# Four operands and 32 bytes: moving the MLP's right operands to another place within 64 bytes

## The chip, the cores and the metric

The kernel runs on one core of a Trainium2 chip. The metric is the device time of one execution in microseconds; the kernel before took 1090.73 us, the median of 3 runs (1088.52 to 1092.98). A profile of one further execution shows what each engine did.

## The reference, cut to what matters

Attention with mixing over heads before and after the softmax, then a block of a low-rank mixing over tokens and an MLP:

```python
B, H, S, D = 4, 12, 448, 64          # attention
scores = q @ k.T / sqrt(D)
scores = einsum('bhij,hg->bgij', scores, w_pre)
attn   = softmax(scores)
attn   = einsum('bhij,hg->bgij', attn, w_post)
x = (attn @ v) as [B, S, 768]
u  = x + (x.T @ U @ V).T             # U 448x32, V 32x448
out = u + relu(u @ w_ch1) @ w_ch2    # w_ch1 768x3072, w_ch2 3072x768
```

U, V and the MLP's weights arrive as 64-bit floats, all else as 32-bit floats.

## The kernel before

The attention works on 16 units of tokens, four for each batch. A unit's scores are made by L381 from k and q, copied out of PSUM into one of three s buffers, and sent by a DMA (the relay, L388) into a tile t that has heads and tokens side by side, where L412 mixes the heads. Softmax, the second mixing (L447) and the product with v (L488, L496) follow, and the result is gathered in acc, one tile for each batch.

The low-rank step transposes acc (L677), multiplies by U (L694, 8 matmuls of 256 columns) and by V (L708, 2 matmuls of 448 columns). Its operands are full-rate 32-bit floats (float32r), split into a high and a low part. The sum u is split likewise into uh and ul, one pair of tiles for each batch.

The MLP takes the hidden dimension in 24 pieces f of 128 and the batches b one after the other. For each (f, b) the up step (L750) makes 18 matmuls: for each of 6 pieces of 128 model channels, low weights by uh, high weights by ul, high weights by uh. Each has 128x128 weights and a right operand of 448 columns, and each has its own weight load. ReLU's result is split into hh and hl (L755, L759), and the down step (L770) makes 3 matmuls for each hidden piece and each 128 output channels, which VectorE adds to acc (L773). 24 x 4 x 18 = 1728 matmuls are up, as many are down. The weights of the next f are loaded, narrowed from 64 to 32 bits by ScalarE, VectorE and GpSimd through kr and tmp buffers, and split meanwhile.

A planner in the kernel (class Plan) simulates the engines with its own costs and due times and writes out the order of all steps; from the third hidden piece on the order of the MLP is written by hand (`lines`). Neither looks at addresses.

SBUF is filled from two sides. Pools of the left side lie one behind another from the bottom, those of the right side from the top downwards, and a pool that is opened after others were closed takes their place. Every tile takes a multiple of 32 bytes in each partition, nearly all of them a multiple of 64. In the built program the right side's first buffer ends 32 bytes below a multiple of 64, and so kr, tmp1, k, u of batches 0 and 1, w0, u of batch 2, h, w0's second buffer, w1 and u of batch 3, which follow each other on that side, all start at 32 mod 64 (at 224 mod 256 too). The tiles of the low-rank step on the left (xh, xl, t3, u4, v4) start at 0 mod 64. The pools are opened by small steps without an engine, for instance:

```python
def open_qk(eng):
    qk_ctx.close()
    for b in range(2):
        open_u(b, "right")
    pool(whole, "w0_0", 1, "right")
```

Tile names in the rows: uh, ul, hh, hl are the right operands; w0h, w0l the up weights, w1h, w1l the down weights; xl, xh with u, and v with t, are the low-rank step's; bank is PSUM.

Of the kernel before, what the change touches and what calls it, by code (L numbers as in the profile page):

```python
# [8 lines left out]
F32 = mybir.dt.float32  # L9
# [233 lines left out]
def build(tc, q2, kt, vj, wpre_in, wpost_in, u_in, v_in, ident, w1j, w2, out, show=None):  # L243
    nc = tc.nc
    whole, tail_ctx, a_ctx, mix_ctx, t1_ctx, t0_ctx, qk_ctx = (ExitStack() for _ in range(7))
    sb = {}

    def pool(ctx, name, bufs, side="left", **kw):
        sb[name] = Pool(ctx.enter_context(tc.tile_pool(name=name, bufs=1, side=side, **kw)), plan.where)
        return sb[name]  # L250
# [26 lines left out]
        pool(mix_ctx, n, BUFS[n])  # L277
    pool(t1_ctx, "t1", 1)
    pool(t0_ctx, "t0", 1)
    for n in ("kr", "tmp1"):  # L280
        pool(whole, n, BUFS[n], "right")
    for n in ("k", "q", "s"):
# [239 lines left out]

    uh, ul = {}, {}

    def open_u(b, side):
        p = pool(whole, f"u{b}", 1, side)
        uh[b], ul[b] = (p.tile([128, KC, S], F32R, e) for e in ("uh", "ul"))
# [5 lines left out]
    def open_qk(eng):  # L533
        qk_ctx.close()
        for b in range(2):
            open_u(b, "right")
        pool(whole, "w0_0", 1, "right")

    def open_t0(eng):
        t0_ctx.close()  # L540
        open_u(2, "right")

    def open_t1(eng):
# [2 lines left out]

    def open_mix(eng):
        mix_ctx.close()
        pool(whole, "w0_1", 1, "right")

    def open_a(eng):
# [2 lines left out]

    def open_tail(eng):
        tail_ctx.close()
        open_u(3, "right")

    plan.add("open_qk", [(None, 0)], open_qk, 0, [("relay", nu - 1, h) for h in range(H)])
    plan.add("open_t0", [(None, 0)], open_t0, 0, ["open_qk"] + [("premix", k) for k in range(first[nu - 2] // 2, (first[nu - 1] + 1) // 2)])  # L560
    plan.add("open_t1", [(None, 0)], open_t1, 0, ["open_t0", ("premix", NC // 2 - 1)])
    plan.add("open_mix", [(None, 0)], open_mix, 0, ["open_t1", ("postmix", NC // 2 - 1)])
    plan.add("open_a", [(None, 0)], open_a, 0, ["open_mix"] + [("av", nu - 2, p) for p in (0, AV)])
    plan.add("open_tail", [(None, 0)], open_tail, 0, ["open_a"] + [("av", nu - 1, p) for p in (0, AV)])

    count = [0]
# [225 lines left out]
    for f in range(KF):  # L792
# [8 lines left out]
        for b in range(B):  # L801
# [9 lines left out]
            n = 1 if (f, b) == (KF - 1, B - 1) else 2  # L811
# [103 lines left out]
```

## Time and profile before

| what | value |
|---|---|
| median of 3 runs | 1090.73 us |
| the profiled execution | 1100.28 us |
| its span, first to last instruction | 1098.5 us |
| mean granted TensorE clock | 0.992 of 2.4 GHz |
| TensorE matmul busy | 1059.1 us |
| VectorE, ScalarE, GpSimd busy | 666.5, 408.4, 271.9 us |
| matmuls at L750 and L770 | 1728 each |

Matmuls overlap in the array, so that the duration of one (368 ns) is longer than the time from one start to the next; that time is read from a count of matmuls in a window, or from a group of the chain of waits divided by its count.

### The profile page before, as it was taken

How to read it: one execution, taken by the hardware profiler on the slowest of the kernel's cores; microseconds unless marked ns; L12 is line 12 of the kernel's file. 1: busy time of each engine (PE TensorE's matmuls, PEld its weight loads, DVE VectorE, ACT ScalarE, POOL GpSimd, SP SyncE). 2: the span in 40 equal slices, each digit the busy share in tenths (PEclk: the TensorE clock that was granted, in tenths of full speed). 3: DMA queues.
4: the chain of work that ended last, by engine and by line, in shares of the span. 5: the costliest groups of instructions: out<-in, count | busy, mean ns of one | idle time of the engine just before them, and what ended most of it. 6: DMA issues, size and time to landing. Idle time of an engine off the chain costs nothing.

```text
span 1098.5 us, 28397 instructions
## 1 busy us (share of the span) xinstructions
PE 1059.1 (96%) x12120; PEld 874.2 (80%) x12120; DVE 666.5 (61%) x1076; ACT 408.4 (37%) x852; POOL 271.9 (25%) x398
## 2 busy tenths in 40 slices
PE   4798999999999999999999999999999999999998
PEld 1365666665666899999999999999999999999997
DVE  0574564565688687665665666565666566566634
ACT  2786677677768721222112212212221211221200
POOL 3131111111224522232222222222222222222200
PEclk8899999999999999999999999999999999999999
DMA  7665646635755211221122212111211211221105
GB/s 277 191 187 171 196 128 193 200 119 167 213 198 163 82 31 44 58 58 58 44 58 58 58 44 58 56 46 58 58 48 53 58 44 57 58 58 44 44 1 200
DMA packets 52270, 108.11 MB, mean 98 GB/s; under 512 B 5056, under 2 KB 38320, under 8 KB 51632
## 3 DMA queue, kind: packets, MB, share of 16 engines
q1 hardware_dynamic: 52144, 106.30, 31.4%
q8 instruction: 95, 1.56, 0.6%
q14 instruction: 31, 0.25, 0.1%
HBM read 57.91 MB, written 7.08 MB: 59 GB/s over the span
## 4 chain that ended last, share of the span: by engine, by line
PE 89%; DMA 4%; ACT 3%; DVE 2%; issue 2%; SPq 0%; POOL 0%; ACTq 0%; DVEq 0%
PE bank L750 33%; PE bank L770 33%; PE bank L447 6%; PE bank L488 5%; PE bank L381 5%; PE bank L412 5%; DMA t<-s 3%; ACT e L422 2%; PE bank L496 1%; DVE mx L417 1%; PE bank L677 1%; PE bank L694 1%; ACT s L299 1%; DMA k<-in_kt 0%; ACT a L299 0%
## 5 line engine op out<-in xcount | busy, mean ns | idle before, releaser
L773 DVE TENSOR_TENSOR acc<-acc,bank 128x896 f32<-128x896 f32 (+1 forms) x153 | 163.5, 1070 | 173.5 <-PE bank L770 172.9
L755 ACT ACTIVATE hh<-bank 128x448 fp32r<-128x448 f32 x96 | 52.4, 546 | 492.2 <-PE bank L750 312.2
L750 PE MATMUL bank<-uh,w0l 128*128 128x448 f32 x576 | 212.2, 368 | 0.0
L770 PE MATMUL bank<-hh,w1l 128*128 128x448 f32 x576 | 212.1, 368 | 0.0
L770 PE MATMUL bank<-hl,w1h 128*128 128x448 f32 x576 | 211.9, 368 | 0.0
L770 PE MATMUL bank<-hh,w1h 128*128 128x448 f32 x576 | 211.9, 368 | 0.0
L750 PE MATMUL bank<-uh,w0h 128*128 128x448 f32 x576 | 211.9, 368 | 0.0
L750 PE MATMUL bank<-ul,w0h 128*128 128x448 f32 x576 | 211.9, 368 | 0.0
L610 POOL TENSOR_TENSOR a<-a,x 128x384 f32<-128x384 f32 (+2 forms) x98 | 98.6, 1006 | 422.6 <-PE bank L750 381.2
L417 DVE TENSOR_REDUCE mx<-bank 128x2 f32<-128x896 f32 x90 | 97.7, 1088 | 69.5 <-PE bank L412 63.7
L447 PEld LDWEIGHTS bank<-wr,e 60*64 60x64 f32 x5040 | 89.4, 135 | 45.8 <-issue 31.9
L422 ACT ACTIVATE e<-bank,mx 128x448 f32<-128x448 f32 x180 | 113.3, 642 | 13.0 <-DVE mx L417 9.2
L770 PEld LDWEIGHTS bank<-hh,w1l 128*128 128x128 f32 x576 | 108.1, 188 | 11.1 <-DVE acc L773 0.3
L770 PEld LDWEIGHTS bank<-hh,w1h 128*128 128x128 f32 x576 | 108.1, 188 | 10.9
L750 PEld LDWEIGHTS bank<-uh,w0l 128*128 128x128 f32 x576 | 108.1, 188 | 10.9
L750 PEld LDWEIGHTS bank<-uh,w0h 128*128 128x128 f32 x576 | 108.1, 188 | 10.9
L770 PEld LDWEIGHTS bank<-hl,w1h 128*128 128x128 f32 x576 | 108.1, 188 | 10.8
L750 PEld LDWEIGHTS bank<-ul,w0h 128*128 128x128 f32 x576 | 108.1, 188 | 10.8
L381 PE MATMUL bank<-k,q 64*64 64x448 f32 (+1 forms) x768 | 96.1, 569 | 15.5 <-ACT s L299 9.0
L759 DVE SCALAR_TENSOR_TENSOR hl<-bank,hh 128x448 fp32r<-128x448 f32 x96 | 59.9, 624 | 81.3 <-ACT hh L755 81.3
L447 PE MATMUL bank<-wr,e 60*64 60x60 f32 x5040 | 93.3, 219 | 8.9 <-issue 6.6
L412 PE MATMUL bank<-t,wpre 64*64 64x448 f32 x720 | 87.6, 557 | 8.8 <-DMA t<-s 5.8
(61 smaller groups left out, 1105.1 us busy)
## 6 DMA issues: line engine op xcount, KB each, us to landing
t<-s SPq DMA_DIRECT2D x192, 210.0 KB
kr<-in_w1j SPq DMA_DIRECT2D x48, 384.0 KB
kr<-in_w SPq DMA_DIRECT2D x48, 384.0 KB
v<-in_vj SPq DMA_DIRECT2D x4, 1536.0 KB
q<-in_q SPq DMA_DIRECT2D x32, 186.0 KB
out<-acc SPq DMA_DIRECT2D x9, 448.0 KB
k<-in_kt SPq DMA_DIRECT2D x4, 672.0 KB
k<-in_kt SPq DMA_DIRECT2D x4, 448.0 KB
```

Of the source, the lines that this page charges most:

```text
L381: eng.matmul(o[at, i, :S], lhsT=q[d, p, at], rhs=k[d, p, :], start=True, stop=True)
L412: eng.matmul(o[64 * j:64 * j + 64, i, :S], lhsT=wpre[64 * i:min(64 * i + 64, QW)], rhs=tt[u % 2][64 * i:min(64 * i + 64, QW), n, :], start ...
L417: eng.tensor_reduce(out=mx, in_=T["pre", k][:, :, :S], axis=AX.X, op=ALU.max, negate=True)
L422: eng.activation(out=e[:, i], in_=T["pre", k][:, i, :S], func=ACTF.Exp, bias=T["mx", k][:, i:i + 1], accum_out=sm[:, i:i + 1])
L447: eng.matmul(d, lhsT=e[64 * j:64 * j + HALF, i, x * KB:x * KB + KB], rhs=wr[64 * j:64 * j + HALF, i].rearrange("p (g m) -> p g m", m=MH), ...
L488: eng.matmul(main[i * D:(i + 1) * D, c, :n], lhsT=v[:, p + c, i, x, :], rhs=a[:, x * H + 2 * (p + c) + i, :n], start=(c == 0 and x == 0), ...
L610: eng.tensor_tensor(out=f32(a), in0=f32(a), in1=f32(x), op=ALU.add)
L750: eng.matmul(ps, lhsT=w[:, c * 128:(c + 1) * 128], rhs=u[:, c, :], start=(i == 0), stop=(i == 3 * KC - 1))
L755: eng.activation(out=hh, in_=T["up", f, b], func=ACTF.Relu)
L759: eng.scalar_tensor_tensor(out=hl, in0=T.pop(("up", f, b)), scalar=0.0, in1=f32(T["hh", f, b]), op0=ALU.max, op1=ALU.subtract)
L770: eng.matmul(ps[:, j, :S], lhsT=w[:, (c + j) * 128:(c + j + 1) * 128], rhs=h, start=(i == 0), stop=(i == len(todo) - 1))
L773: eng.tensor_tensor(out=two(b, c, n), in0=two(b, c, n), in1=T.pop(("dn", f, b, c))[:, :n, :S], op=ALU.add)
```

## The change

Five pools of 32 bytes (8 floats in each partition) are opened on the right side. The first lies below everything there, so that all of it moves down by 32 bytes; the others stand between right operands and weights. In the built program u of all batches and the six h pairs start at 0 mod 64 bytes and w0 and w1 still at 32. By the same pads kr, tmp1 and k come to 0 mod 64 (from 32), the three s buffers to 32 (from 0), and the three q buffers to 32, 0, 32 (from 0, 32, 0). Nothing on the left side moves. Every engine has the same instructions in the same order, with the same waits.

```diff
     pool(t0_ctx, "t0", 1)
+    pool(whole, "shift0", 1, "right").tile([128, 8], F32, "shift")
     for n in ("kr", "tmp1"):
         pool(whole, n, BUFS[n], "right")
...
+    def shift(n):
+        pool(whole, f"shift{n}", 1, "right").tile([128, 8], F32, "shift")
+
...
         for b in range(2):
             open_u(b, "right")
+        shift(1)
         pool(whole, "w0_0", 1, "right")
 
     def open_t0(eng):
         t0_ctx.close()
+        shift(2)
         open_u(2, "right")
...
         mix_ctx.close()
+        shift(3)
         pool(whole, "w0_1", 1, "right")
...
         tail_ctx.close()
+        shift(4)
         open_u(3, "right")
```

## Rows read from the trace of the kernel before

**Rows 1.** The page's first part: busy us (share of the span) xinstructions.

```profile
PE 1059.1 (96%) x12120; PEld 874.2 (80%) x12120; DVE 666.5 (61%) x1076; ACT 408.4 (37%) x852; POOL 271.9 (25%) x398
```

**Rows 2.** The page's chain that ended last, shares of the span by line.

```profile
PE bank L750 33%; PE bank L770 33%; PE bank L447 6%; PE bank L488 5%; PE bank L381 5%; PE bank L412 5%; DMA t<-s 3%; ACT e L422 2%; PE bank L496 1%; DVE mx L417 1%; PE bank L677 1%; PE bank L694 1%; ACT s L299 1%; DMA k<-in_kt 0%; ACT a L299 0%
```

**Rows 3.** The same chain in order of time: start us, us, what.

```profile
367.26 3.84 PE bank L750 x18
...
372.89 3.91 PE bank L750 x18
...
385.93 0.95 PE bank L694 x8
...
388.10 0.87 PE bank L677 x8
388.98 0.41 PE bank L708 x2
...
392.01 3.72 PE bank L750 x18
...
396.68 3.66 PE bank L750 x18
...
401.22 0.40 PE bank L708 x2
401.62 3.65 PE bank L770 x18
...
409.11 4.96 PE bank L770 x24
414.06 14.88 PE bank L750 x72
...
1073.74 21.09 PE bank L770 x102
```

**Rows 4.** One window: length, busy us (x) by engine, TensorE clock, DMA share, GB/s.

```profile
414.00:1094.00 680.00, 680.00 (x3292) 617.66 (x3291) 413.02 (x671) 133.16 (x263) 173.27 (x171) 1.00 0.19 57
```

**Rows 5.** One form, 420 to 1090 us: count, busy us, mean ns, idle before.

```profile
L770 PE MATMUL bank<-hh,w1h 128*128 128x448 f32 x544 | 200.2, 368 | 0.0
```

**Rows 6.** Timeline of the last matmuls: start us, us, engine line op.

```profile
1094.04 0.37 PE L770 MATMUL bank<-hh,w1l 128*128 128x448 f32 x1
1094.04 0.19 PEld L770 LDWEIGHTS bank<-hl,w1h 128*128 128x128 f32 x1
1094.25 0.37 PE L770 MATMUL bank<-hl,w1h 128*128 128x448 f32 x1
1094.25 0.19 PEld L770 LDWEIGHTS bank<-hh,w1h 128*128 128x128 f32 x1
...
1094.45 0.37 PE L770 MATMUL bank<-hh,w1h 128*128 128x448 f32 x1
```

**Rows 7.** Weight loads by line: ns min/median/max, first and last start us.

```profile
L750 PEld LDWEIGHTS bank<-ul,w0h x576: 187/188/192, 367.3 to 1073.0; 128*128 128x128 f32 x192
L694 PEld LDWEIGHTS bank<-xl,u x48: 186/188/193, 126.5 to 405.3; 112*128 112x128 f32 x48
L708 PEld LDWEIGHTS bank<-v,t x24: 186/189/192, 132.3 to 408.5; 128*128 128x128 f32 x24
```

**Rows 8.** Timeline of TensorE where an up group is followed by L694.

```profile
385.15 0.37 PE L750 MATMUL bank<-uh,w0l 128*128 128x448 f32 x1
385.35 0.37 PE L750 MATMUL bank<-ul,w0h 128*128 128x448 f32 x1
385.56 0.37 PE L750 MATMUL bank<-uh,w0h 128*128 128x448 f32 x1
385.76 0.64 PE L694 MATMUL bank<-xl,u 112*128 112x256 f32 x4
```

**Rows 9.** Waits for relays: engine, line, waited for, us, times, longest us.

```profile
ACT s L299 <- DMA t<-s: 22.5, 13, 10.0
PE bank L412 <- DMA t<-s: 5.8, 1, 5.8
```

## The prediction

> **What bounds the kernel now.** I read first the page's busy times and its chain of waits, then that chain in order of time, then the steady stretch as one window, and last the timeline where one kind of matmul follows another.
>
> TensorE is busy 96% of the span [rows 1], and two matmul lines, L750 (up) and L770 (down), hold 33% each of the chain that ended last [rows 2]. From about 409 us to the end the chain is nothing but these two lines, one group after the other [rows 3]: the reader is to see that no transfer and no other engine stands between them. The window from 414 to 1094 us says the same in one row: 3292 matmuls in 680.0 us, TensorE busy all of it at a granted clock of 1.00 (the 2.4 GHz level), VectorE busy 413.0 us, ScalarE 133.2, GpSimd 173.3 [rows 4]. A row of one form has no idle time before it [rows 5]. So the last 62% of the span lasts as long as 3292 matmuls take from start to start, and the change can only matter much if it changes that pace.
>
> The pace: a group of 18 takes 3.72 us and 72 take 14.88 us [rows 3], 206.7 ns each. A matmul streams 448 columns, and at 2.4 GHz they need 448 / 2.4 = 186.7 ns. 20.0 ns of each matmul, 3292 x 20.0 = 65.8 us in the window, are neither columns nor waits for another engine. That is the whole stake: the question is whether these 20 ns come from where the operands lie.
>
> **The change part by part.** The program issues the same instructions in the same order with the same waits; only addresses differ. Nothing is added to any engine or queue, no wait is added or removed, and no DMA moves. Three things get other places.
>
> *The MLP's right operands u and h* go from 32 to 0 mod 64 bytes, its weights stay at 32. Three readings of the trace bear on the price.
>
> First, pace without any change of place. All MLP groups before have both operands at 32, and yet two paces occur: 18 matmuls in 3.65 or 3.66 us at 401.62 and 396.68, in 3.72 from 392.01 and from 414 us on; and two groups that both start cold, at 367.26 and 372.89, last 3.84 and 3.91, again 0.07 apart [rows 3]. So 202.8 ns is possible with the old alignment, and the trace falls into the slower pace at 406 to 409 us and keeps it. What it falls into is decided by something finer than these addresses.
>
> Second, pace with both operands at 0. The low-rank step's matmuls (L694) read both operands at 0 mod 64: 8 of 256 columns take 0.95 us [rows 3], 118.8 ns each, 0.464 ns a column against 206.7 / 448 = 0.461 in the MLP. Two of L708, 448 columns and both at 0, take 0.41 and 0.40 us [rows 3], 200 to 205 ns each. Putting the right operand at 0 has not removed the excess there. In these rows the weights lie at 0 as well, so the mixed case stands in no long row.
>
> Third, the weight load. If load and stream disturbed each other, a matmul beside which no load runs would be shorter. The last matmul, at 1094.45, has no load after it, and it still took 0.37 us like the ones before it, each of which has the next load starting with it [rows 6]. Loads take 188 or 189 ns at the median whether the weights lie at 32 (L750) or at 0 (L694, L708) [rows 7]. So a conflict between the two operands, which is what a mixed alignment would cure, is not what the excess looks like. Only short mixed pieces exist: the L750 matmul that starts at 385.56, right operand at 32, runs beside the load of L694's weights at 0, and is followed after 0.20 us; the two before it are followed after 0.20 and 0.21 [rows 8]. At two decimals that is no difference.
>
> The Trainium skill, page "SBUF — State Buffer", section "Who interferes with whom", says that TensorE reads the streamed operand and the weights through two independent ports and waits on no one; that the last matmul is no shorter agrees with it. By that rule the pads do nothing.
>
> From both sides: nothing at one end. At the other, count 64-byte pieces: 448 floats are 1792 bytes, 28 pieces from 0 but 29 touched from 32; if the pace went with pieces touched it would be 206.7 x 28 / 29 = 199.6 ns, 7.1 x 3292 = 23.4 us less. The loss side is bounded among the rivals. Between them I take nothing, since the rows at 0 (0.464 ns a column) stand nearer to the old pace than to a better one, and the last matmul has the old length without the supposed partner.
>
> *The attention stage's buffers.* The three s buffers go from 0 to 32 mod 64, the q buffers swap 0 and 32, k goes from 32 to 0. Relays t<-s hold 3% of the chain [rows 2], 33 us, and ScalarE and TensorE wait 22.5 and 5.8 us for them [rows 9]. If a row of 28 pieces cost a twenty-eighth more, that is +1.2 us. The score matmuls (L381), 5% of the chain or 56 us, read k from 0 now: by the same count -1.9 us. Float32 matmuls of this stage show no sign of alignment: the transposes of L677 take weights at steps of 1800 bytes, so at every eighth of a 64-byte piece, and 8 take 0.87 us, 109 ns each [rows 3]; that is 128 columns at half the rate, 2 x 128 / 2.4 = 106.7, and 2 ns, so that only streams at the full rate carry the large excess. Taken as 0, with -2 to +1 as ends.
>
> *Staging buffers kr and tmp1* go from 32 to 0. They are written by DMA and read by VectorE, ScalarE and GpSimd, which have 267 us of slack or more in the window [rows 4]; these cost nothing, and would only if VectorE's work there grew by more than half (680 / 413 = 1.65).
>
> **Sum.** The profiled execution took 1100.28 us, its span 1098.5, so 1.8 lie outside; the timed runs have a median of 1090.73 (1088.52 to 1092.98). Changes are taken off that median. 0 for the MLP, -2 to +1 for attention: 1090 us, with an own range of 1086 to 1095. From the spread of the three runs, about 0.4%, this kernel's measurement can't tell less than 0.5%, 5.5 us, from no change.
>
> **Rivals.** *The quicker pace lasts.* The steady stretch takes whichever pace its first matmuls fall into; other addresses could tip it to 202.8 ns, or make it the only one. For it: the quicker pace is in the trace for whole groups, and of the two the stretch has the slower now, so that a tip between them can only gain. Against it: the same addresses hold both, so addresses need not decide. Price: 3.72 - 3.65 = 0.07 us per 18, x 3292 / 18 = 12.8 us, 1078 us; with 28 pieces instead of 29, 1067. VectorE, with 413 us of work, would still not bound the 667 us that are left.
>
> *The excess goes altogether.* If the equal halves were the whole cause, 65.8 us go: 1025. For it: the excess is the same in every matmul, as something structural would be. Against it: rows with both operands at 0 and the lone last matmul. The Trainium skill, page "TensorE: Matmul & The Clock Gate", section "Back-to-back issue gap", gives N / 2.4 + 2.5 ns between matmuls at the full clock, 189.2 ns here; by that the saving would be 17.5 x 3292 = 57.6 us and the time 1033. The measured 206.7 doesn't agree with it for this operand type, before any change.
>
> *Slower: stream and load now meet.* With right operand and weights in different halves of a 64-byte piece, a load that so far found its half free may hold the stream up. It costs from the first such meeting, at L750 and L770 alike, since TensorE has no idle time there; the load by itself has 206.7 - 188 = 19 ns before it sets the pace. One piece per matmul is 16 columns x 0.461 = 7.4 ns, x 3292 = 24 us: 1115; one in three matmuls gives 1099. For it: the mix stands in no long row, so nothing excludes it. Against it: single mixed pieces in rows 8 are not longer, and loads have the same length at either place.
>
> **How the numbers follow.** No change 0.43; the quicker pace 0.34; the excess gone 0.06; slower 0.17. The likeliest gives 1090. Faster by over 0.5% is 0.34 + 0.06 = 0.40, within 0.43, slower 0.17. The range 1066 to 1098 holds the first two cases to the end of 28 pieces and the lightest part of the slower one (0.04); it leaves out 0.06 and 0.13.
>
> **What would show it.** In the profile after, the window of the steady stretch tells all: about 486 matmuls per 100 us is no change, 493 the quicker pace, 501 the piece count, 535 no excess, and under 484 the slower rival. A group of 18 at 3.72 us in the chain says the same. The relays' waits should stay near 22.5 us, and the stretch before 367 us should keep its length within 2 us. I am wrong if the pace in the steady stretch is not 206 to 207 ns; whether L694 and L708, which the change doesn't touch, then keep theirs tells if the mix did it or a shift in time.

## The result and the profile after

The changed kernel took 1095.21 us at the median of 20 runs, the kernel before, run beside it, 1090.24 us. The ratio is 1.0051 with a 95% interval of 1.003 to 1.0072: slower by half a per cent, a little beyond what I called no change, and not the 1090 us that I forecast. The time lies inside the range, the direction does not fit. Single executions far outside the rest (2643.79 us of the kernel before and 1841.92 of the changed one here, 3617.97 in e1, 4120.58 in e4) are not in the ratios.

The two profiled executions hide this: their spans are 1098.5 and 1098.6 us. Lines after the change stand 1 to 8 lower in the file: L758 is the up step (L750 before), L778 the down step (L770), L702 and L716 the low-rank step (L694, L708), L413 the head mixing (L412). L685 is the transposes (L677). The page after, busy times and then the chain by line, to be held against [rows 1] and [rows 2]:

```profile
PE 1056.1 (96%) x12120; PEld 880.0 (80%) x12120; DVE 666.3 (61%) x1076; ACT 408.5 (37%) x852; POOL 272.9 (25%) x398
...
PE bank L778 32%; PE bank L758 32%; PE bank L448 5%; PE bank L489 5%; PE bank L413 5%; PE bank L382 5%; DMA t<-s 4%; ACT e L423 1%; PE bank L497 1%; PE bank L685 1%; ACT s L300 1%; DVE mx L418 1%; PE bank L702 1%; DMA q<-in_q 1%; ACT a L300 0%
```

The shape is the same: TensorE bounds, and the steady stretch is one group of matmuls after another. One window of it, columns as in [rows 4]:

```profile
424.00:1084.00 660.00, 660.00 (x3226) 605.54 (x3225) 404.54 (x661) 132.87 (x263) 174.10 (x171) 1.00 0.19 54
```

660.0 us / 3226 = 204.6 ns a matmul, where [rows 4] gives 206.6. (A count takes in the matmuls that the window's edges cut, so a pace read from it comes out up to 0.1 ns below one read from a group.) So in this pair of traces the MLP gained: the first up group starts at 373.99 us (367.26 in [rows 3]) and the end is the same within 0.1 us, 6.7 us lost ahead of it and 6.6 won in it. The chain in order of time shows that there is no longer one pace:

```profile
373.99 3.92 PE bank L758 x18
...
379.69 3.81 PE bank L758 x18
...
408.27 3.60 PE bank L778 x18
...
415.70 4.96 PE bank L778 x24
...
500.47 4.81 PE bank L778 x24
...
511.42 3.62 PE bank L758 x18
515.04 4.95 PE bank L778 x24
...
534.80 3.72 PE bank L758 x18
...
559.40 4.81 PE bank L778 x24
...
570.35 3.62 PE bank L758 x18
573.98 4.95 PE bank L778 x24
```

24 matmuls take 4.81 us (200.4 ns each) in one group and 4.95 (206.3) in another, 18 take from 3.60 to 3.72, and the pattern comes again after 58.93 us (500.47 and 559.40), which is two hidden pieces.

If both traces were typical, the kernels would be equal. They aren't, by 20 runs each. Either the attention stage loses more in most executions, or the trace of before isn't typical. The experiments were to tell these apart.

### The profile page after: what moved, and what is told of

It is laid out like the page before. It is cut to its first block, busy times and chain, and to the rows that moved or that the text cites. A ratio compares the mean times of both kernels' runs of the same rounds, so it can differ in the third digit from the quotient of the medians.

```text
span 1098.6 us, 28397 instructions
## 1 busy us (share of the span) xinstructions
PE 1056.1 (96%) x12120; PEld 880.0 (80%) x12120; DVE 666.3 (61%) x1076; ACT 408.5 (37%) x852; POOL 272.9 (25%) x398
## 4 chain that ended last, share of the span: by engine, by line
PE 88%; DMA 5%; ACT 3%; issue 2%; DVE 2%; SPq 1%; ACTq 0%; POOL 0%; DVEq 0%
PE bank L778 32%; PE bank L758 32%; PE bank L448 5%; PE bank L489 5%; PE bank L413 5%; PE bank L382 5%; DMA t<-s 4%; ACT e L423 1%; PE bank L497 1%; PE bank L685 1%; ACT s L300 1%; DVE mx L418 1%; PE bank L702 1%; DMA q<-in_q 1%; ACT a L300 0%
## 5 line engine op out<-in xcount | busy, mean ns | idle before, releaser
L778 PE MATMUL bank<-hh,w1l 128*128 128x448 f32 x576 | 211.6, 367 | 0.0
L758 PE MATMUL bank<-ul,w0h 128*128 128x448 f32 x576 | 211.5, 367 | 0.0
L778 PE MATMUL bank<-hh,w1h 128*128 128x448 f32 x576 | 211.4, 367 | 0.0
L778 PE MATMUL bank<-hl,w1h 128*128 128x448 f32 x576 | 211.4, 367 | 0.0
L758 PE MATMUL bank<-uh,w0h 128*128 128x448 f32 x576 | 211.1, 367 | 0.0
L758 PE MATMUL bank<-uh,w0l 128*128 128x448 f32 x576 | 211.0, 366 | 0.0
L758 PEld LDWEIGHTS bank<-uh,w0l 128*128 128x128 f32 x576 | 108.1, 188 | 10.1
L778 PEld LDWEIGHTS bank<-hh,w1l 128*128 128x128 f32 x576 | 108.2, 188 | 9.9 <-DVE acc L781 0.3
L778 PEld LDWEIGHTS bank<-hh,w1h 128*128 128x128 f32 x576 | 108.2, 188 | 9.8
L778 PEld LDWEIGHTS bank<-hl,w1h 128*128 128x128 f32 x576 | 108.2, 188 | 9.7
L758 PEld LDWEIGHTS bank<-ul,w0h 128*128 128x128 f32 x576 | 108.1, 188 | 9.6
L758 PEld LDWEIGHTS bank<-uh,w0h 128*128 128x128 f32 x576 | 108.1, 188 | 9.4
L382 PE MATMUL bank<-k,q 64*64 64x448 f32 (+1 forms) x768 | 98.4, 577 | 17.0 <-ACT s L300 10.2
L413 PE MATMUL bank<-t,wpre 64*64 64x448 f32 x720 | 88.7, 558 | 8.6 <-DMA t<-s 6.3
```

The costliest lines, as they stand in the source:

```text
L382: eng.matmul(o[at, i, :S], lhsT=q[d, p, at], rhs=k[d, p, :], start=True, stop=True)
L413: eng.matmul(o[64 * j:64 * j + 64, i, :S], lhsT=wpre[64 * i:min(64 * i + 64, QW)], rhs=tt[u % 2][64 * i:min(64 * i + 64, QW), n, :], start ...
L758: eng.matmul(ps, lhsT=w[:, c * 128:(c + 1) * 128], rhs=u[:, c, :], start=(i == 0), stop=(i == 3 * KC - 1))
L778: eng.matmul(ps[:, j, :S], lhsT=w[:, (c + j) * 128:(c + j + 1) * 128], rhs=h, start=(i == 0), stop=(i == len(todo) - 1))
```

## Experiments

**The kernel before again (e1).** No edit.

> The kernel before, unchanged, for the scatter of its pace and of its attention stage. Theory A (the places act in both stages): the steady window holds 486 matmuls per 100 us again, the MLP starts at 367 us within 1 us, time ratio 1.000. Rival B (each execution falls into a pace and into clock drops by chance): the pace may be 493 per 100 us this time, or the MLP starts 3 us or more away from 367.2 us.

Ratio 0.999 (0.9958 to 1.0022), times from 1083.6 to 1104.0 us. The same program, profiled with a span of 1082.2 us, 16.3 shorter than the trace that I had predicted from. First the window of the steady stretch in this second trace of before (columns as in [rows 4]), then its chain in order of time where that stretch begins (start us, us, what):

```profile
414.00:1074.00 660.00, 660.00 (x3259) 611.58 (x3258) 409.60 (x666) 132.18 (x263) 173.34 (x171) 1.00 0.20 57
```

```profile
403.30 2.44 PE bank L770 x12
405.74 0.41 PE bank L708 x2
406.15 4.87 PE bank L770 x24
411.02 13.98 PE bank L750 x69
```

660 / 3259 = 202.5 ns, and 13.98 / 69 = 202.6 where [rows 3] have 14.88 / 72 = 206.7 at the same place in the program. The quick pace of [rows 3], there in single groups, lasts here to the end. Rival B's first half is shown: an execution of the kernel before falls into one of two paces.

**The change again (e2).** No edit.

> The changed kernel, unchanged. Theory A: the MLP starts near 374 us again (367.2 before), the steady window has about 489 matmuls per 100 us, time ratio 1.005. Rival B: the start of the MLP scatters by several us and may lie at 367 us, and the TensorE clock drop at 283 us of its first trace is not there; ratio 1.00 within 0.3%.

Ratio 1.007 (1.0043 to 1.0096), so the loss is there again. Its window has one matmul more than that of the first trace after:

```profile
424.00:1084.00 660.00, 660.00 (x3227) 605.46 (x3226) 407.49 (x663) 132.06 (x262) 172.31 (x169) 1.00 0.19 56
```

**One part alone (e3, e4).** e3 keeps the attention stage's pads and puts all MLP operands back to 32 mod 64; e4 does the opposite. Against the changed kernel:

```diff
 e3: open_qk
         qk_ctx.close()
+        shift(1)
         for b in range(2):
             open_u(b, "right")
-        shift(1)
 (and no shift(2), shift(3), shift(4))
 e4: build and open_qk
-    pool(whole, "shift0", 1, "right").tile([128, 8], F32, "shift")
         qk_ctx.close()
+        shift(0)
```

> Only the attention stage's part: k, q, s, kr and tmp1 lie as after, u, h and the weights all at 32 mod 64 as before. Theory A: MLP start near 374 us, pace 206.7 ns as before, so about 7 to 11 us slower than before, ratio 1.007 to 1.010. Rival B: ratio 1.00 within 0.3%.

> Only the MLP's part: u and h at 0, weights at 32 mod 64 at the same addresses as after; k, q, s, kr and tmp1 as before. Theory A: MLP start near 367 us, pace 204.6 ns, so about 6.6 us faster than before, ratio 0.994. Rival B (the loss comes with the new MLP places or by chance): ratio 1.005 as the whole change.

e3 had 1.0128 (1.0093 to 1.0162), e4 1.0073 (1.0039 to 1.0107). Theory A, a loss in attention and a gain in the MLP, falls with e4: the MLP's pads alone cost as much as the whole change, within the intervals. And e3's number, a little over the 1.007 to 1.010 that theory A had foretold, comes from elsewhere, as the same window of its trace says:

```profile
414.00:1074.00 660.00, 660.00 (x3196) 599.48 (x3195) 400.45 (x657) 132.31 (x263) 173.63 (x171) 1.00 0.19 52
```

Its first up group starts at 366.1 us, no later than before; its MLP runs at 660 / 3196 = 206.5 ns. The execution of e4 that was profiled is the one of 4120.58 us, so its trace can't tell the pace; what the MLP's pads alone do is read from its times.

**Attention by itself (e5, e6).** 4 of the 24 hidden pieces, so that the pace of the MLP hardly counts; e5 from the kernel before, e6 from the changed one.

```diff
-KC, KF = DM // 128, DFF // 128
+KC, KF = DM // 128, 4
```

> The kernel before with 4 of the 24 hidden pieces (20 pieces left out, the order of all else the same), so that attention and the low-rank step hold some three quarters of the time; a pace of 202.7 or 206.7 ns changes it by 2 us at most. About 490 us. Theory A (the attention buffers' places cost time): the times lie within 3 us of each other. Rival B (attention scatters by itself): they scatter by 8 us or more, as the whole kernel's do.

> The changed kernel with 4 of the 24 hidden pieces, otherwise as it is. Theory A: 6 to 10 us above the short kernel before (first up at 370 to 374 us in two traces against 364 to 367). Rival B: the same median within 2 us, and the difference of those traces was chance. A third theory C (the loss sits in the MLP): the same too.

508.62 us (500.71 to 513.53) and 507.46 (504.91 to 514.15): as ratios to the full kernel before 0.4626 (0.4595 to 0.4658) and 0.4639 (0.4618 to 0.4661). I had expected about 490. The 6 to 10 us of theory A are not there; a cost of up to some 5 us could hide in the two intervals. The short kernel scatters by some 10 us by itself, and nearly all of that is attention's. The 6.7 us ahead of the MLP in the first pair of traces lie within that scatter.

**The MLP by itself (e7 to e16).** 72 hidden pieces, the 24 three times over, so that a nanosecond a matmul is worth 10 us.

```diff
-KC, KF = DM // 128, DFF // 128
+KC, KF = DM // 128, 72
+NF = DFF // 128
-            src = (w1j[f], w2[f * 128:(f + 1) * 128, :])[i // 2]
+            src = (w1j[f % NF], w2[f % NF * 128:(f % NF + 1) * 128, :])[i // 2]
```

> The kernel before with the 24 hidden pieces three times over (72 pieces, 10368 MLP matmuls, so the output is another). About 364 + 3 x 714 to 727 us. If each execution falls into 202.7 or 206.7 ns by chance and keeps it, the times stand in two heaps about 40 us apart, near 2510 and 2550 us. If the pace wanders within an execution, they lie in between and close together.

> The changed kernel with 72 hidden pieces. Theory A: both traces had 204.69 ns, so all executions lie within 8 us of each other, near 2530 us, between the two heaps of the long kernel before. Theory C (the changed MLP is slower than most executions before): its median lies 5 us or more over the long kernel before. Rival B: two heaps here too.

e7, before: 2487.1, 2487.6, 2490.9, 2491.9, 2493.6 and, alone, 2531.9 us, two heaps 40 us apart as expected, each some 20 us below the time that I had given. The profile is of that last one; of a quick execution of e7 there is none. e8, changed: 2504.4 to 2508.5 and one of 2517.2, one heap between those two. The same window of both, e7 first and then e8:

```profile
600.00:2400.00 1800.00, 1800.00 (x8711) 1634.70 (x8710) 1104.47 (x1815) 367.30 (x726) 490.53 (x484) 1.00 0.19 54
```

```profile
600.00:2400.00 1800.00, 1800.00 (x8799) 1651.79 (x8798) 1116.17 (x1834) 369.26 (x732) 496.51 (x488) 1.00 0.19 54
```

206.6 ns before, in the execution of 2531.9 us, and 204.6 after. The chain of e8 shows the same two kinds of group as the first trace after (L779 is its down step):

```profile
609.86 4.81 PE bank L779 x24
...
624.44 4.95 PE bank L779 x24
```

This is theory C: by the times, the changed MLP runs at the mean of its groups in every execution, the kernel before at the quick pace in five of six (4.0 ns x 10368 matmuls are 41.5 us, the distance of the heaps).

The pads of the others, in bytes ahead of u of batches 0 and 1, w0, u of batch 2, w0's second buffer, u of batch 3, with the first one opened in open_qk as in e4:

```diff
 e9  (e3's pads)            all operands at 160 mod 256
 e10 32                     all at 192
 e11 32, 32, 96, 32, 96     right 64, weights 32 mod 128
 e12 32, 96, 32, 96, 32     right 64, weights 96 mod 128
 e13 0, 32, 32, 32, 32      right 32, weights 0 mod 64
 e14 128                    all at 96 mod 256
 e15 96                     all at 128 mod 256
 e16 32                     all at 192, and on the left side:
+    pool(whole, "shiftl", 1).tile([128, 24], F32, "shift")
     for n in ("tmp2", "xn", "t3"):
```

> The kernel with the attention stage's places of after and every MLP operand at 32 mod 64 (32 mod 128), 72 hidden pieces in place of 24. Theory D (where all operands lie alike, an execution keeps the pace it falls into; where the places differ from tile to tile, each change of tiles knocks it out of one): two heaps, near 2490 and 2530 us, like the long kernel before. Its 24-piece form was 1.3% slow, so if its places make the slow pace the rule, all lie near 2530. Rival E (the pace follows from halves alike or different): as the long kernel before, most near 2490.

> 72 hidden pieces, one pad of 32 bytes ahead of u, so that right operands and weights all lie at 0 mod 64 (64 mod 128); attention as before. Theory D: every execution keeps one pace, 202.7 or 206.7 ns, times near 2490 or 2530 us. If the number of 64-byte pieces that a right operand touches (28 instead of 29) counted, the pace were 199.6 ns and the time near 2460 us. Rival E: halves alike, so as the long kernel before.

> 72 hidden pieces, right operands at 0 and weights at 32 mod 64 as in the change, but with pads that put all right operands at 64 mod 128 and all weights at 32 mod 128 (in the change they are at 0 or 64, and at 32 or 96). Theory D: no more knocks, one pace is kept through an execution, 200 ns (2464 us), 202.7 (2490) or 206.7 (2530). Rival E: 204.7 ns, 2505 us, as the long changed kernel.

> The same with all right operands at 64 and all weights at 96 mod 128. Theory D: one pace kept through an execution, 200 ns (2464 us), 202.7 (2490) or 206.7 (2530), not necessarily that of the one before. Rival E: 204.7 ns, 2505 us.

> 72 hidden pieces, the mirror of the change: right operands at 32, weights at 0 mod 64. If different halves knock the stream out of a pace at each change of tiles, whichever lies where: about 204.7 ns, 2505 to 2515 us, no two heaps. If only the weights' being at 32 matters: one kept pace, 2490 or 2530 us.

> 72 hidden pieces, all MLP operands moved by 128 bytes from the kernel before, so alike and at 96 mod 256 (96 mod 128 and 32 mod 64, as before). If the place within 128 bytes decides which pace is kept: as the long kernel before, most near 2490 us. If the place within 256 bytes or the entry decides: all near 2530 us.

> 72 hidden pieces, all MLP operands alike and at 128 mod 256, which is also where the low-rank step's operands lie. One pace kept through an execution; 2530 us if only the place of before has the quick pace, 2490 if the entry from operands at the same place leads into it.

> 72 hidden pieces, MLP operands alike at 192 mod 256 (all of six runs slow in that place), and the low-rank step's operands moved by 96 bytes so that the distance from them to the MLP's is that of the kernel before, mod 128. If the entry from the low-rank step decides: most near 2490 us. If the MLP's own place decides: all near 2530 us.

| run | right, weights | median us (lowest to highest of 6) | matmuls in 600 to 2400 us |
|---|---|---|---|
| e9 | alike, 160 | 2533.32 (2530.22 to 2535.41) | 8712 |
| e10 | alike, 192 | 2530.70 (2529.18 to 2534.39) | 8712 |
| e14 | alike, 96 | 2534.16 (2529.66 to 2538.69) | 8712 |
| e15 | alike, 128 | 2486.91 (2485.47 to 2493.52) | 8883 |
| e16 | alike, 192, left side moved | 2488.40 (2485.48 to 2495.28) | 8884 |
| e11 | different halves | 2514.26 (2507.80 to 2522.68) | 8790 |
| e12 | different halves | 2511.52 (2507.90 to 2513.65) | 8792 |
| e13 | different halves, mirrored | 2510.25 (2506.18 to 2513.92) | 8799 |

Three things follow. First, with operands alike, one of the two paces is kept for over 2 ms, whatever the place; with different halves no trace shows one kept and no time lies in either heap, and the mean is 204.6 to 204.8 ns, also where the residues mod 128 are the same in all groups (e11, e12; there theory D, that only differences from tile to tile knock the stream out, was wrong) and also in the mirror. Read from start to start in blocks of 36 matmuls, from the low-rank step to the end, the traces of e7, e9, e10 and e14 stay between 206.3 and 206.7 ns, those of e15 and e16 between 202.6 and 202.8; e8 and e13 go from 201.8 to 206.7, e11 from 202.2 to 206.7 and e12 from 204.1 to 205.4. In e12 the groups differ too (L759 up, L779 down; 203.3 to 205.0 ns):

```profile
604.66 2.46 PE bank L779 x12
607.12 3.69 PE bank L759 x18
610.80 4.92 PE bank L779 x24
615.72 3.66 PE bank L759 x18
```

In every run that is called alike the operands have the same place mod 256. None has them in the same half of 64 bytes and at different places mod 128 or 256, so it isn't shown whether it is the halves or any difference of place that keeps the stream from a pace. Second, 0 or 32 mod 64 is not what counts: e10 at 0 has the slow pace, e15 at 0 the quick one. Third, e10 and e16 have their MLP operands at the same addresses and stand 42 us apart, with no run of either in the other's heap. e16 differs in what lies on the left side, the low-rank step's operands among it. The two ran on different chips. The chip is a poor rival: the kernel before took 1087.74 us at the median beside e10 and 1097.78 beside e16, which is the other way round, and e14 ran beside e15 and e16 on one chip and was slow in six of six. Their windows, e10 first:

```profile
600.00:2400.00 1800.00, 1800.00 (x8712) 1634.74 (x8711) 1103.63 (x1814) 365.10 (x726) 492.03 (x484) 1.00 0.19 54
```

```profile
600.00:2400.00 1800.00, 1800.00 (x8884) 1668.41 (x8883) 1125.40 (x1851) 372.24 (x741) 501.06 (x494) 1.00 0.20 55
```

and the chain where the low-rank step ends and the steady stretch begins, e10 first (L775 and L776 are the down step, L713 and L714 the product by V):

```profile
408.11 2.44 PE bank L775 x12
410.55 0.40 PE bank L713 x2
410.95 4.96 PE bank L775 x24
```

```profile
404.61 2.47 PE bank L776 x12
407.08 0.41 PE bank L714 x2
407.49 4.86 PE bank L776 x24
```

In e10 the 12 down matmuls ahead of the last two of the low-rank step are quick (203 ns), the 24 behind them slow (207); in e16 it is the other way round (206 and 203). In the kernel before, the pace passes this place as it is: e1 has 2.44, then 4.87 (above), and the first trace has

```profile
406.22 2.47 PE bank L770 x12
408.69 0.41 PE bank L708 x2
409.11 4.96 PE bank L770 x24
```

So a pace can turn into the other where the kind of matmul changes, and the one that stands after the last change is kept; what stands ahead of the MLP is part of it. Addresses alone don't settle it, since the kernel before has both outcomes. The distance between the two steps' operands doesn't settle it by a simple rule: it is 96 mod 128 in e14 and in e16, which differ.

**At full length (e17, e18).** The placements of e15 and e16 in the kernel with 24 pieces.

> The full kernel with one pad of 96 bytes ahead of u, so that all MLP operands lie alike at 128 mod 256, as the low-rank step's do; attention as before. If the way in decides the pace: 202.7 ns in every run, no run of the slow heap, 1082 to 1092 us, ratio 0.994 to 0.999 (the kernel before is quick in part of its runs). If the long form's pace was chance: as the kernel before, ratio 1.000.

> The full kernel with MLP operands alike at 192 mod 256 and all left-side tiles after acc moved by 96 bytes. If the way in decides: 202.7 ns, 1082 to 1092 us, ratio 0.994 to 0.999. If the MLP's place decides (six of six slow without the move on the left): 206.7 ns, 1096 to 1106 us, ratio about 1.01.

1087.33 us, ratio 0.9984 (0.9954 to 1.0014), and 1086.18 us, 0.9981 (0.9952 to 1.0011). Both traces have the quick pace, in the window of e17 and then of e18:

```profile
420.00:1080.00 660.00, 660.00 (x3258) 611.60 (x3257) 409.27 (x665) 132.36 (x263) 173.50 (x171) 1.00 0.20 57
```

```profile
414.00:1074.00 660.00, 660.00 (x3258) 611.60 (x3257) 409.32 (x665) 132.20 (x263) 173.23 (x171) 1.00 0.20 56
```

e18's interval leaves out the 1.01 that I expected if the MLP's own place decided; the same kernel without the move on the left was not run at full length. Both intervals hold 1: where the kernel before is quick in most executions anyway, there is little left to win, and neither is shown to beat it.

## Why the prediction was wrong

**The steps that failed: "0 for the MLP" in the sum, and "The pace" that it was judged by.** The changed MLP runs at 204.7 ns a matmul where the kernel before, quick, runs at 202.7: the term put at 0 is 2.0 x 3456 = 6.9 us against a quick execution. Measured were 0.0051 x 1090.24 = 5.6 us (3.3 to 7.8), and 7.6 in e2. The text couldn't see the sign, since it read 206.7 ns from one execution and made the whole stake from it. That execution was in the slow pace; five of six of e7 are, by their times, in the quick one. The sign was on the table: the profiled execution took 1100.28 us, the median of the runs is 1090.73, and I wrote both down and took "changes off that median" without asking what 9.55 us were. The two paces differ by 206.67 - 202.67 = 4.0 ns, or 13.2 us over 3292 matmuls, enough for that with attention's scatter on top.

How large the loss is hangs on how often the kernel before is quick. Beside e13 to e16, on one chip, 6 of its 11 runs lie above 1097 us and the median is 1097.78, against 1087.74 to 1093.36 in the other comparisons. The changed kernel wasn't run at full length there, so that it is slower on every chip is not shown.

**"Of the two the stretch has the slower now, so that a tip between them can only gain."** True of the trace, wrong of the kernel, for the same reason. With it fell the direction of the rival that I gave 0.34.

**"From both sides: nothing at one end."** This is where the 0 came from. The mixed places do act: in e8, e11, e12 and e13 no trace keeps a pace. I had argued from rows with both operands at 0 and from a matmul beside which no load runs, and said that the mixed case stands in no long row; that open place held the effect. The first of these arguments stands for what it says, that 0 by itself brings no better pace: e10 and e15 have both at 0 and 206.6 and 202.6 ns. The second read a duration to two decimals, and the mean duration of a matmul differs by 3 ns between the paces (368 ns before, 365 in e1), so it could not show a change of this size; nor could the single mixed pieces of [rows 8]. The rule from the Trainium skill, page "SBUF — State Buffer", section "Who interferes with whom", by which TensorE waits on no one, and from which I took that the pads do nothing, didn't give the result; no run here shows whether a wait at the memory is behind it.

**The count of 64-byte pieces, 199.6 ns.** Groups at 200.4 ns are in the trace after, so that this pace exists, but e15 and e10, both with 28 pieces, run at 202.6 and 206.6. The count doesn't set it.

**The slower rival** had the sign, with a mechanism (a load holds the stream up, 7.4 ns a matmul) and prices of 8 and 24 us that the runs don't show: no group in the steady stretch after is slower than the slow pace of before.

**Attention at 0, staging buffers at 0** hold as far as the runs can tell: e5 and e6 show no cost of attention's places beyond their scatter, and e9, with kr and tmp1 moved, has as many matmuls in its window as e10, where they are not (8712). Waits for relays in the first trace after are 24.0 and 6.3 us, against 22.5 and 5.8 in [rows 9]:

```profile
ACT s L300 <- DMA t<-s: 24.0, 12, 10.2
PE bank L413 <- DMA t<-s: 6.3, 1, 6.3
```

**What would show it.** The pace in the steady stretch, 204.6 ns, is the text's own sign of being wrong. Its other test says the mix did it: in the first trace after, 8 matmuls of L702 take 0.94 to 0.96 us and 2 of L716 0.40 or 0.41, as L694 and L708 did. The stretch ahead of the MLP grew by 6.7 us in that trace where 2 were allowed, which is scatter. One number was not on the footing of the others: 486 for no change is a count with the matmuls at the edges in it, 493, 501 and 535 are 100 us through the pace, and so no change is 484.

What stays open is what inside the chip makes the paces. The runs show when one is kept and that what runs ahead of the MLP is part of what settles which; they don't show why 448 columns take 200.4 to 206.7 ns and not 186.7. The Trainium skill, page "TensorE: Matmul & The Clock Gate", section "Back-to-back issue gap", gives N / 2.4 + 2.5 ns as the gap of an isolated matmul at the full clock, 189.2 ns for 448 columns, and says that in a stream of loads and matmuls it over-counts at large N. The traces disagree: every pace here lies above it.

## What to carry to other kernels

Compare the time of the profiled execution with the median of the runs before any number is taken from its trace; where they differ by about the effect in question, the trace is of one kind of execution and a second trace is worth more than a finer reading of the first. A stretch that one engine holds for hundreds of microseconds can have more than one stable pace, as here, and an edit that moves only addresses can change how often each comes up, so compare distributions and multiply the stretch to see them apart. Don't expect one place to be the better one: with operands alike two placements gave 2487 and 2488 us, three gave 2531 to 2534 and that of the kernel before gave both, with operands in different halves it was 2506 to 2514 each time. If the pace matters, try placements of what runs just ahead of the stretch as well as of its own operands.

## What the runs showed of the hardware

Streams of full-rate 32-bit matmuls of 448 columns, each with its own 128x128 weight load, ran at the 2.4 GHz level (granted clock 1.00) at 206.7 or 202.6 ns a matmul where all operands have the same place mod 256 bytes, and kept it through 10,000 matmuls; with right operands and weights in different 32-byte halves of 64 bytes groups ran from 200.4 to 206.7 ns, 204.6 to 204.8 on average. One program (e7) took 2487 to 2494 us in five executions and 2532 in a sixth, which had the slow pace. With the MLP's operands at the same addresses and other tiles moved by 96 bytes, the median of six executions went from 2530.70 us (e10) to 2488.40 (e16, on another chip), and the six of each lie within 10 us. What inside the chip makes the paces is not shown.
